# Float32 scores in pairs of heads from head 18 on, and another order of the opening phase

## The chip, the cores and the metric

The kernel runs on one core of one Trainium2 chip. The metric is the device time of one execution in microseconds (us), here the median of three runs. A profiled execution is a run of its own, and its time is given beside the median.

## What is computed

Three blocks follow one another: causal attention over blocks of 64 positions (8 batches, 8 heads, 576 positions, 64 features a head), a mixer block (a rank-32 mixing over positions, then a two-layer perceptron of width 2048 with a residual), and a gated output block.

```python
scores = scale * q @ k.T                      # per head, 576 x 576, blocks above the diagonal masked
attn = softmax(scores); x = attn @ v          # heads side by side: (8, 576, 512)
u = x + ((x.T @ U) @ V).T                     # mixing over positions
x = u + relu(u @ w_ch1) @ w_ch2               # 512 -> 2048 -> 512
gate = sigmoid(causal_conv5(x, conv_w))
out = (gate * (x @ w_val)) @ w_out
```

q, k, v are float32; the weights `w_ch1` and `w_ch2` come in 64 bits and are turned into pairs of float32 values in the kernel.

## The kernel before

**Stages.** The 64 heads (8 batches of 8) are numbered n. Phase 1 handles attention alone, for heads 0 to 10, and the mixing of batch 0. Then come nine groups of 512 tokens, each with 16 steps f of the perceptron: `emit_h1` (12 matmuls of 512 columns, lines 854 to 872) and `emit_o` (12 matmuls, lines 874 to 903). Each of them calls `gap()` twice, and `gap()` takes some steps of the attention stream for the heads of the next batch. The last stage is the gated output block (from 1329 us on).

**The attention stream.** `attention()` runs `tick(n)` for each head: four pieces of the scores (`emit_q_bank` for n under `NQ` = 18, `emit_s_piece` from 18 on), the maximum, then the product with v of head n-2 (`emit_pv`), the exponentials, and `emit_est` of head n-1. A pair of heads is normed in `emit_norm_a/b` and mixed by `mix_T`, `mix_G` and `mix_H` at fixed delays (`TPOS`, `GPOS`, `HPOS`; for batch 0 `T0`, `G0`, `H0`).

**Scores from head 18 on.** `prep_qk` (line 368) makes from the transposed tq and tk of a head three single-pass (float32r) operands: `ks` (the high part of k on both halves of the partitions), `kl` (its low part, the other half zero) and `qs` (high and low part of q). That is three ACT copies, one POOL memset and two POOL subtractions of 64x576 a head. `emit_s_piece` then does two float32r matmuls over all 128 rows for each part, into one PSUM bank, and one ACT copy (line 402) to SBUF. A float32 matmul, as in `emit_q_bank` (line 432) and for heads under 18 in `emit_pv` (line 612), appears in the trace as two MATMUL instructions.

**PSUM.** Four banks (`ps_p`) hold in turn everything but the four accumulators of `emit_o`: h1, the score pieces, the product with v, transposes and mixing. The order of TensorE's instructions is that of the program; the other engines' order is set at build time by priority, where an earlier line goes first and `tc.high_priority()` lifts what is inside.

**Weight blocks.** 32 calls of `split_w1` and `split_w2` (line 799 on) load 512 KB each, turn it to float32 on ACT, DVE (lines 124, 126, 127, 145: tile `wa`) and POOL, and for w2 store it again. Four of them (`PRE` = 2) are issued ahead of the first head, ten come in phase 1 at every 8th step of the stream, the other 18 in group 0, two a step f.

Of the kernel before, what the change touches and what calls it, by code (L numbers as in the profile page):

```python
# [8 lines left out]
F32 = mybir.dt.float32  # L9
F32R = mybir.dt.float32r  # L10
# [7 lines left out]
P = 128  # L18
# [4 lines left out]
def attn_moe_gate_kernel(ctx: ExitStack, tc: tile.TileContext, q, k, v, U, V, w1, w2, wval, convw, wout, out):  # L23
# [25 lines left out]
    LEAD = 2  # L49
    GATE = True  # L50
    GATE0 = False
    C0 = 6
    C1 = 8
    CMAX = 32
    LOWP = 0
    ABUF = 4
    RAWB = 2
    WAB = 2
    QV = 10
    KV = 0  # L60
    UVE = 0
    HPOS = 8
    GPOS = 6
    TPOS = 5
    PRE = 2
    CV0 = 1
    CV1 = 3
    MX0 = 0
    TP0 = 0
    NR0 = 0  # L70
    MM0 = 0
# [1 line left out]
    PR0 = 0  # L73
    CWAIT = 4
    NQ = FIRST_SPLIT
    MORE = 1
    T0 = 5
    G0 = 7
    H0 = 9
    NPART = 0  # L80
    PAT = (0,1)
    URG = True
# [4 lines left out]
    def f32(ap):  # L87
        return ap if ap.dtype == F32 else ap.bitcast(F32)
# [3 lines left out]
    def hi_act(o, i):  # L92
        act.copy(o, i)  # L93
# [4 lines left out]
    def lo(eng, o, i, h):  # L98
        eng.tensor_tensor(o, i, f32(h), op=ALU.subtract)  # L99
# [204 lines left out]
    def setup_att():  # L304
        for t in vstk:
            pool.memset(t[:, :, D:P], 1.0)
            pool.memset(t[0:D, NK - 1, :], 0.0)
        for a in range(2):
            for t in kz:
                pool.memset(t[a][own[1 - a]], 0.0)  # L310

    raw = {}

# [23 lines left out]
    stk = {}  # L337

    own = [slice(0, D), slice(D, P)]
    def pads(nm, dtype):  # L340
        return [st_p.tile([P, S], dtype, tag=f"{nm}{a}", name=f"{nm}{a}") for a in range(2)]

    kz = [pads(nm, F32) for nm in ("ks", "qs")]
    ks, qs = [], []
    kl = st_p.tile([P, S], F32R, name="kl")
    qkt = {}

    def prep_t(pn):
        if pn >= B * NP:
            return  # L350
        t = raw.pop(pn)
        if 2 * pn < NQ:
            tq = rot("tk" if pn % 2 else "tq", 1)
            z = kz[pn % 2]
            for rows in own if pn == 0 else (slice(0, P),):
                vec.transpose(tq[rows], t["q"][rows])
                for a in range(2):
                    if pn or rows == own[a]:
                        vec.transpose(z[a][own[a]], t["k"][own[a]])
            qkt[pn] = (tq, z)  # L360
        else:
            tq, tk = rot("tq", 1), rot("tk", 1)
            vec.transpose(tq, t["q"])
            vec.transpose(tk, t["k"])
            qkt[pn] = (tq, tk)
        load_qk(pn + 1)

    def prep_qk(n):
        if n >= B * H or n < NQ:
            return  # L370
        if not ks:
            ks.extend(pads("ks", F32R))
            qs.extend(pads("qs", F32R))
        tq, tk = qkt[n // 2]
        a = n % 2
        me, ot = own[a], own[1 - a]
        hi_act(qs[a][me], tq[me])
        hi_act(ks[a][me], tk[me])
        hi_act(ks[a][ot], tk[me])
        pool.memset(f32(kl[ot]), 0.0)  # L380
        lo(vec if n < KV else pool, kl[me], tk[me], ks[a][me])
        lo(vec if n < QV else pool, qs[a][ot], tq[me], qs[a][me])

    def kslice(j):
        return slice(q0[j], q0[j] + P) if q0[j] + P <= S else slice(S - P, S)

    stt = {}

    def emit_s_piece(n, i):
        pr, a = divmod(n, 2)  # L390
        if i == 0:
            stt[n] = [s_p.tile([P, w], F32, tag=f"s{h}", name=f"s{h}") for h, w in enumerate(sw)]
        ps = psum["a"].tile([P, 512], F32, tag="a", name="pS")
        o = 0
        for j, a0, a1 in pieces[i]:
            w = a1 - a0
            pe.matmul(ps[:, o:o + w], ks[a][:, kslice(j)], qs[a][:, a0:a1], start=True, stop=False)  # L397
            pe.matmul(ps[:, o:o + w], kl[:, kslice(j)], qs[a][:, a0:a1], start=False, stop=True)  # L398
            o += w
        j, a0, a1 = pieces[i][0]  # L400
        d = soff[j] + a0 - q0[j]
        act.copy(stt[n][half_of[j]][:, d:d + o], ps[:, 0:o])  # L402


    qbanks = [
# [14 lines left out]
    def emit_q_bank(n, i):  # L420

        a = n % 2
        tq, z = qkt[n // 2]
        if i == 0:
            s0, s1 = (s_p.tile([P, w], F32, tag=f"s{h}", name=f"s{h}") for h, w in enumerate(sw))
            eqs[n] = {3: s0[:, 0:4 * P], 1: s0[:, 4 * P:6 * P], 0: s1[:, 0:P], 2: s1[:, P:4 * P], 4: rot("m" if a else "mb", 1)}
            t = tiny_p.tile([P, 2 * NTT + 2], F32, tag="rq", name="rq")
            qmax[n] = (t[:, 0:NTT + 1], t[:, NTT + 1:], psum["a"].tile([P, 512], F32, tag="a", name="pS"))
        r, nm, _ = qmax[n]
        ps = psum["a"].tile([P, 512], F32, tag="a", name="pS") if i else _  # L430
        for t, k0, k1, o in qbanks[i]:
            pe.matmul(ps[:, o:o + k1 - k0], tq[:, kslice(t)], z[a][:, k0:k1], start=True, stop=True)
        if i == 0:
            vec.memset(ps[0:D, 4 * P - D:4 * P], MASKED)
        elif i == 2:
            vec.memset(ps[0:D, 3 * P - D:3 * P], MASKED)
        elif i == 3:
            vec.memset(ps.rearrange("p (c w) -> p c w", w=D)[0:D, 1:6:4, :], MASKED)
        for t, k0, k1, o in qbanks[i]:
            c = t + (k0 > 0)  # L440
            vec.reduce_max(r[:, c:c + 1], ps[:, o:o + k1 - k0], axis=AX.X)
        if i == 0:
            x = vec.tensor_scalar(nm[:, 3:4], r[:, 3:4], -scale, None, op0=ALU.mult)
        elif i == 2:
            vec.tensor_tensor(r[:, 4:5], r[:, 4:5], r[:, 5:6], op=ALU.max)
            x = vec.tensor_scalar(nm[:, 2:5:2], r[:, 2:5:2], -scale, None, op0=ALU.mult)
        elif i == 3:
            x = vec.tensor_scalar(nm[:, 0:2], r[:, 0:2], -scale, None, op0=ALU.mult)
        if i == 1:
            eqs[n]["wait"] = ps  # L450
            return
        noted(1, x)
        noted(3, x)
        for t, k0, k1, o in qbanks[i] + (qbanks[1] if i == 2 else []):
            src = eqs[n]["wait"] if i == 2 and t == NTT - 1 and k0 == 0 else ps
            act.activation(eqs[n][t][:, k0:k1], src[:, o:o + k1 - k0], AF.Exp, bias=nm[:, t:t + 1], scale=scale)
# [95 lines left out]
    def emit_est(n):  # L552

        if not 0 <= n < NH:
            return
        if n < NQ:
            emit_q_turn(n)
            return
        ss = stt.pop(n)
        for half, s in enumerate(ss):  # L560
            skip = 0 if half else WHOLE
            if half == 0:
                ef = late["e"].tile([P, WHOLE], F32, tag="ef", name="ef")
                act.activation(ef, s[:, 0:WHOLE], AF.Exp, scale=scale)
            eh = late["e"].tile([P, sw[half] - skip], F32R, tag=f"eh{half}", name="eh")
            hi_act(eh, s[:, skip:])
            el = e_p.tile([P, sw[half]], F32R, tag=f"e{half}", name="el")[:, skip:]
            lo(vec, el, s[:, skip:], eh)
            est[n, half] = (eh, el, ef, skip)
# [128 lines left out]
    def mix_H(pn, i):  # L698
        pcs = mix_pieces(pn // NP)
        if i >= len(pcs):  # L700
            return
        gi, a0, a1, off = pcs[i]
        if gi >= 2 and gi > y_done[0] + 2:
            later.append((pn, i))
            return
        xt = xts[pn]
        d = pn % NP
        uh, ul = u_tiles(gi)
        w = a1 - a0
        ps = ps_p.tile([P, 512], F32, tag="a", name="pH")  # L710
        pe.matmul(ps[:, 0:w], gst[pn], vst[:, a0:a1], start=True, stop=True)
        with behind(MX0 if pn < NP else 0):
            vec.tensor_tensor(xt[:, a0:a1], ps[:, 0:w], xt[:, a0:a1], op=ALU.add)
        hi_act(uh[:, d, off:off + w], xt[:, a0:a1])
        lo(pool, ul[:, d, off:off + w], xt[:, a0:a1], uh[:, d, off:off + w])
# [7 lines left out]
    def tick(n, mixed, last=B * NP):  # L723
# [5 lines left out]
        load_v(e + 1)  # L729
        for i in range(4):  # L730
            if n < NQ:
                emit_q_bank(n, i)
            elif new:
                emit_s_piece(n, i)
            if i == 3 and new and n >= NQ:
                emit_corners(n)
                emit_max_a(n)
            yield
        if new:
            if n >= NQ:  # L740
                emit_max_b(n)
            if n % 2 == 1:
                prep_t((n + 1) // 2)
            prep_qk(n + 1)
        yield from mixing(2 * e, mixed, last)
        if new and n >= NQ:
            for _ in emit_max_c(n):
# [261 lines left out]

    load_qk(0)  # L1010
    act.activation(cw[0:1, 0, 0:1], unit[0:1, 0:1], AF.Exp)
    for f in range(PRE):
        split_w1(f)
        split_w2(f)
    setup_att()
    prep_t(0)
    prep_qk(0)
    pb1 = ExitStack()
    pbp = {}

# [13 lines left out]
        pbp["ps"] = pb1.enter_context(tc.tile_pool(name="pbps", bufs=2, space=PSUM, side="right"))  # L1034

    stream = attention()
    convs = [(fn, f) for f in range(PRE, NF) for fn in (split_w1, split_w2)]

    def conv(n):
        where[0] = CV0 if gated_conv[0] else CV1  # L1040
# [131 lines left out]
```

## Time and profile before

| | us |
|---|---|
| median of 3 runs (1531.53 to 1535.98) | 1533.32 |
| the profiled execution | 1538.09 |
| its span, first to last instruction | 1536.3 |
| first perceptron matmul | 127.5 |
| start of group 1 | 314.9 |
| end of attention, about | 1154 |
| start of the gated output block | 1329 |

A row of the chain or the timeline gives start, duration, engine, line, operation, output<-inputs, shape and count; what stands in brackets is how long the engine sat idle before, and what ended that. In a row of stretches the stretch's length is followed by each engine's busy time, the granted TensorE clock (1.00 is 2.4 GHz, half of it 1.2 GHz) and the share of the DMA engines.

### The profile page before, as it was taken

Reading aid. Unit: us, or ns where it says so; the run is one execution under the profiler, and the core shown is the slowest. Engines: PE = TensorE matmul, PEld = TensorE weight load, DVE = VectorE, ACT = ScalarE, POOL = GpSimd, SP = SyncE. Lnnn points to the kernel's source line nnn. Section 1 sums busy time; section 2 is a strip of 40 time slices with the busy share of each in tenths; the row PEclk is TensorE's granted clock in tenths of the full one; section 3 lists DMA queues with packets and bytes.
Section 4 is the critical chain, followed back from the end, with each engine's and each line's share of the span. In section 5 each row is a group of like instructions: output and inputs, shape, how many; then the busy total and the mean of one; then the engine's idle time right before and its main releaser. Section 6 shows DMA issues by size and latency. Waiting matters only on the chain. (4 is left out here: it accounts for less than half of the span.)

```text
span 1536.3 us, 20391 instructions
## 1 busy us (share of the span) xinstructions
PE 1427.0 (93%) x6664; PEld 1151.1 (75%) x6664; DVE 1146.3 (75%) x2252; ACT 789.5 (51%) x1639; POOL 516.1 (34%) x587
## 2 busy tenths in 40 slices
PE   5897899979989998999899989989999999999999
PEld 2665677868767787777687778768888888778887
DVE  7887874659887888788888878887624427399991
ACT  4785565546565665666476556655512212243432
POOL 3133232333435333534443444335104210353410
PEclk8998999989999999999999999999999999999999
DMA  7555662224233333333323333232225543323221
GB/s 171 142 133 167 204 194 79 79 80 103 79 81 114 85 86 105 92 79 89 109 79 90 92 92 93 78 85 90 77 83 198 174 135 123 105 68 103 78 74 69
DMA packets 246291, 163.58 MB, mean 106 GB/s; under 512 B 197669, under 2 KB 212261, under 8 KB 246186
## 3 DMA queue, kind: packets, MB, share of 16 engines
q1 hardware_dynamic: 246186, 162.29, 36.6%
q8 instruction: 53, 0.87, 0.2%
q14 instruction: 52, 0.43, 0.1%
HBM read 134.98 MB, written 27.26 MB: 106 GB/s over the span
## 5 line engine op out<-in xcount | busy, mean ns | idle before, releaser
L887 PE MATMUL acc<-hh,w 128*128 128x512 f32 x1152 | 408.4, 405 | 10.2 <-ACT hh L869 10.2
L887 PEld LDWEIGHTS acc<-hh,w 128*128 128x128 f32 x1152 | 220.7, 192 | 57.7 <-ACT hh L869 12.8
L841 PE MATMUL h<-uh,w1hi 128*128 128x512 f32 x576 | 239.1, 415 | 9.9 <-DVE hl L870 6.3
L887 PE MATMUL acc<-hl,w 128*128 128x512 f32 x576 | 230.2, 400 | 5.9 <-DVE hl L870 5.9
L841 PE MATMUL h<-uh,w1lo 128*128 128x512 f32 x576 | 228.2, 396 | 0.0
L841 PE MATMUL h<-ul,w1hi 128*128 128x512 f32 x576 | 228.0, 396 | 0.0
L870 DVE SCALAR_TENSOR_TENSOR hl<-h,hh 128x512 fp32r<-128x512 f32 x144 | 98.2, 682 | 116.1 <-ACT hh L869 115.4
L869 ACT ACTIVATE hh<-h 128x512 fp32r<-128x512 f32 x144 | 85.8, 596 | 154.3 <-PE h L841 147.4
L550 ACT ACTIVATE s<-s 128x448 f32<-128x448 f32 x92 | 65.5, 712 | 150.0 <-DVE s L528 149.0
L841 PEld LDWEIGHTS h<-uh,w1hi 128*128 128x128 f32 x576 | 110.7, 192 | 35.8 <-DVE hl L870 8.2
L402 ACT COPY s<-pS 128x320 f32<-128x320 f32 (+2 forms) x184 | 89.8, 490 | 80.9 <-PE pS L398 77.2
L887 PEld LDWEIGHTS acc<-hl,w 128*128 128x128 f32 x576 | 110.5, 192 | 27.5 <-DVE hl L870 8.2
L841 PEld LDWEIGHTS h<-uh,w1lo 128*128 128x128 f32 x576 | 109.7, 190 | 24.8
L841 PEld LDWEIGHTS h<-ul,w1hi 128*128 128x128 f32 x576 | 110.7, 192 | 18.3 <-issue 1.4
L528 DVE TENSOR_TENSOR s<-s,mb 128x64 f32<-128x64 f32 (+4 forms) x230 | 123.0, 598 | 1.3
L962 DVE SCALAR_TENSOR_TENSOR gt<-yb,cw,gt 128x516 f32<-128x516 f32 (+1 forms) x144 | 116.5, 839 | 1.4
L99 POOL TENSOR_TENSOR vlo<-vstk,vhi 128x320 fp32r<-128x320 f32 x46 | 54.3, 1180 | 161.1 <-ACT vhi L93 148.1
L99 POOL TENSOR_TENSOR yl<-yb,yh 128x512 fp32r<-128x512 f32 (+7 forms) x64 | 67.7, 1091 | 96.9 <-ACT yh L93 96.8
L99 POOL TENSOR_TENSOR ul<-xt,uh 128x512 fp32r<-128x512 f32 (+7 forms) x64 | 53.2, 840 | 132.6 <-ACT uh L93 131.9
L397 PE MATMUL pS<-qs,ks 128*128 128x320 f32 (+4 forms) x276 | 80.4, 309 | 6.3 <-ACT lt L614 4.2
L398 PE MATMUL pS<-qs,kl 128*128 128x320 f32 (+4 forms) x276 | 82.4, 302 | 0.0
L99 DVE TENSOR_TENSOR el<-s,eh 128x448 fp32r<-128x448 f32 x92 | 76.7, 859 | 5.2 <-issue 4.6
(152 smaller groups left out, 3105.5 us busy)
## 6 DMA issues: line engine op xcount, KB each, us to landing
w<-w_s SPq DMA_DIRECT2D x144, 512.0 KB, 3.2
rawq<-in_q_dram SPq DMA_DIRECT2D x128, 72.0 KB, 2.4
rawk<-in_k_dram SPq DMA_DIRECT2D x128, 72.0 KB, 2.5
out_dram<-ot SPq DMA_DIRECT2D x35, 256.0 KB, 2.0
raw<-in_moe_w_ch_dram SPq DMA_DIRECT2D x64, 128.0 KB, 2.3
raw<-in_moe_w_ch_dram SPq DMA_DIRECT2D x16, 512.0 KB, 4.2
vstk<-in_v_dram SPq DMA_DIRECT2D x64, 128.0 KB, 2.6
w_s<-wo SPq DMA_DIRECT2D x16, 512.0 KB, 3.6
```

What stands on the lines that cost most here:

```text
L99: eng.tensor_tensor(o, i, f32(h), op=ALU.subtract)
L397: pe.matmul(ps[:, o:o + w], ks[a][:, kslice(j)], qs[a][:, a0:a1], start=True, stop=False)
L398: pe.matmul(ps[:, o:o + w], kl[:, kslice(j)], qs[a][:, a0:a1], start=False, stop=True)
L402: act.copy(stt[n][half_of[j]][:, d:d + o], ps[:, 0:o])
L528: noted(3, vec.tensor_tensor(sv(n, j), sv(n, j), mb[:, q0[j]:], op=ALU.subtract))
L550: act.activation(s, s, AF.Exp, scale=scale)
L841: pe.matmul(ps[:, 0:n], w[:, d, fs], x[:, d, 0:n], start=(d == 0 and i == 0), stop=(d == ND - 1 and i == 2))
L869: act.activation(hh[:, 0:n], ps[:, 0:n], AF.Relu)
L870: latest[0] = vec.scalar_tensor_tensor(hl[:, 0:n], ps[:, 0:n], 0.0, f32(hh[:, 0:n]), op0=ALU.max, op1=ALU.subtract)
L887: pe.matmul(acc[d][:, 0:n], w[:, wi, ds], x[:, 0:n], start=(f == 0 and i == 0), stop=(f == NF - 1 and i == 2))
L962: vec.scalar_tensor_tensor(gt[d][:, 0:gw], y[:, d, j:j + gw], cw[:, d, j:j + 1], gt[d][:, 0:gw], op0=ALU.mult, op1=ALU.add)
```

## The change

From head 18 on the scores are float32 matmuls over 64 rows: head 2p on partitions 0 to 63, head 2p+1 on 64 to 127, in turn for each part, each head into a bank of its own. All four pieces of both heads are issued in the tick of the even head; the odd head's tick has none, and starts its corners and maximum in its first step. `prep_qk` is gone. The score tiles of every third head lie in the buffers `za` and `zb`, which earlier hold the zero-padded k. The chain of `emit_q_bank` and `emit_q_turn` and the add in `mix_H` get high priority. No weight block is issued ahead of the first head; in phase 1 one comes at step 4 and then at every 12th step. Phase 1 has 12 heads (`MORE` = 2), and the mixing of batch 0 (`T0`, `G0`, `H0` = 4, 6, 7) lies wholly inside its ticks.

```diff
-    C0 = 6
-    C1 = 8
+    C0 = 4
+    C1 = 12
-    PRE = 2
-    MORE = 1
-    T0 = 5
-    G0 = 7
-    H0 = 9
+    MORE = 2
+    T0 = 4
+    G0 = 6
+    H0 = 7
...
-    def emit_s_piece(n, i):
-        pr, a = divmod(n, 2)
+    def emit_s_piece(pn, i):
+
+        heads = (2 * pn, 2 * pn + 1)
+        tq, tk = qkt[pn]
         if i == 0:
-            stt[n] = [s_p.tile([P, w], F32, tag=f"s{h}", name=f"s{h}") for h, w in enumerate(sw)]
-        ps = psum["a"].tile([P, 512], F32, tag="a", name="pS")
+            for n in heads:
+                stt[n] = [spare(("za", "zb")[h], w) if n % 3 == 1 else s_p.tile([P, w], F32, tag=f"s{h}", name=f"s{h}") for h, w in enumerate(sw)]
+        ps = [psum["a"].tile([P, 512], F32, tag="a", name="pS") for _ in own]
         o = 0
         for j, a0, a1 in pieces[i]:
             w = a1 - a0
-            pe.matmul(ps[:, o:o + w], ks[a][:, kslice(j)], qs[a][:, a0:a1], start=True, stop=False)
-            pe.matmul(ps[:, o:o + w], kl[:, kslice(j)], qs[a][:, a0:a1], start=False, stop=True)
+            for t, me in zip(ps, own):
+                pe.matmul(t[:, o:o + w], tk[me, kslice(j)], tq[me, a0:a1], start=True, stop=True)
             o += w
         j, a0, a1 = pieces[i][0]
         d = soff[j] + a0 - q0[j]
-        act.copy(stt[n][half_of[j]][:, d:d + o], ps[:, 0:o])
+        for n, t in zip(heads, ps):
+            act.copy(stt[n][half_of[j]][:, d:d + o], t[:, 0:o])
...
         if n < NQ:
-            emit_q_turn(n)
+            with tc.high_priority():
+                emit_q_turn(n)
...
-        with behind(MX0 if pn < NP else 0):
+        with tc.high_priority():
             vec.tensor_tensor(xt[:, a0:a1], ps[:, 0:w], xt[:, a0:a1], op=ALU.add)
...
             if n < NQ:
-                emit_q_bank(n, i)
-            elif new:
-                emit_s_piece(n, i)
-            if i == 3 and new and n >= NQ:
+                with tc.high_priority():
+                    emit_q_bank(n, i)
+            elif new and n % 2 == 0:
+                emit_s_piece(n // 2, i)
+            if i == (0 if n % 2 else 3) and new and n >= NQ:
                 emit_corners(n)
                 emit_max_a(n)
...
-            prep_qk(n + 1)
...
-    for f in range(PRE):
-        split_w1(f)
-        split_w2(f)
-    prep_qk(0)
-    convs = [(fn, f) for f in range(PRE, NF) for fn in (split_w1, split_w2)]
+    convs = [(fn, f) for f in range(NF) for fn in (split_w1, split_w2)]
```

## Rows read from the trace of the kernel before

**Rows 1.** The page: busy time of TensorE, and its busy tenths in 40 slices.

```profile
PE 1427.0 (93%) x6664; PEld 1151.1 (75%) x6664; DVE 1146.3 (75%) x2252; ACT 789.5 (51%) x1639; POOL 516.1 (34%) x587
PE   5897899979989998999899989989999999999999
```

**Rows 2.** Stretches: length; busy PE, PEld, DVE, ACT, POOL; clock, DMA share, GB/s.

```profile
0.00:36.50 36.50, 17.57 (x52) 9.91 (x53) 28.14 (x63) 15.32 (x30) 10.77 (x22) 0.86 0.75 173
36.50:118.50 82.00, 75.52 (x380) 51.53 (x379) 71.58 (x218) 63.13 (x155) 21.24 (x19) 1.00 0.56 141
...
127.50:190.00 62.50, 52.11 (x210) 38.68 (x209) 51.13 (x105) 34.02 (x70) 19.30 (x15) 0.89 0.67 200
...
314.90:1154.00 839.10, 783.37 (x3801) 649.73 (x3800) 673.71 (x1316) 482.12 (x987) 323.00 (x395) 0.98 0.32 89
```

**Rows 3.** Timeline of TensorE from 20 to 41 us.

```profile
21.76 4.41 PE L432 MATMUL pS<-ks,tq 128*128 128x512 f32 x10 [8.04 <-DVE ks L359]
...
32.45 4.19 PE L432 MATMUL pS<-qs,tk 128*128 128x512 f32 x10 [3.79 <-ACT m L456]
36.48 2.98 PE L612 MATMUL pPV<-e,vstk 128*128 128x128 f32 x12
39.29 0.38 PE L472 MATMUL pE<-ident,m 128*128 128x128 f32 x2
```

**Rows 4.** DVE's work on the weight blocks (tile wa) in three stretches: length, busy time.

```profile
0.00:36.50 36.50, 13.61 (x21) 0.86 0.75 173
36.50:118.50 82.00, 23.26 (x47) 1.00 0.56 141
127.50:220.00 92.50, 42.04 (x66) 0.92 0.68 203
```

**Rows 5.** Timeline of TensorE from 118 to 128 us, the end of phase 1.

```profile
122.04 1.44 PE L688 MATMUL pG<-x,ust 128*128 128x256 f32 x5 [3.25 <-DVE x L99]
126.90 0.82 PE L711 MATMUL pH<-vst,g 128*128 128x512 f32 x2 [3.42 <-DVE g L99]
```

**Rows 6.** Timeline of TensorE from 520 to 528 us: score pieces between perceptron matmuls.

```profile
521.13 0.19 PE L397 MATMUL pS<-qs,ks 128*128 128x64 f32 x1
...
521.81 0.39 PE L887 MATMUL acc<-hh,w 128*128 128x512 f32 x1
522.04 0.40 PE L887 MATMUL acc<-hl,w 128*128 128x512 f32 x1
...
524.88 0.37 PE L397 MATMUL pS<-qs,ks 128*128 128x448 f32 x1
...
525.29 0.40 PE L841 MATMUL h<-uh,w1hi 128*128 128x512 f32 x1
```

**Rows 7.** Timeline of TensorE around the only matmuls over few rows (5 rows).

```profile
1179.23 0.39 PE L887 MATMUL acc<-hh,w 128*128 128x512 f32 x1
1179.55 0.41 PE L277 MATMUL pC<-unit,wa 5*128 5x5 f32 x4
1179.89 0.50 PE L841 MATMUL h<-uh,w1hi 128*128 128x512 f32 x1
1180.23 0.40 PE L841 MATMUL h<-ul,w1hi 128*128 128x512 f32 x1
```

**Rows 8.** Groups of instructions by form: work of `prep_qk` (busy us, mean ns).

```profile
L99 POOL TENSOR_TENSOR qs<-tq,qs 64x576 fp32r<-64x576 f32 x46 | 70.4, 1531 | 27.1 <-PE pPV L612 18.9 <-ACT qs L93 5.7
L99 POOL TENSOR_TENSOR kl<-tk,ks 64x576 fp32r<-64x576 f32 x46 | 65.8, 1431 | 9.3 <-ACT ks L93 6.2
L93 ACT CAST ks<-tk 64x576 fp32r<-64x576 f32 x92 | 61.7, 671 | 8.5 <-PE pS L397 6.0 <-DVE tk L364 1.4
```

**Rows 9.** Line 516, a DVE copy of 32x18: least, median and greatest ns.

```profile
L516 DVE COPY r<-r x46: 166/168/1904, 285.3 to 1093.6; 32x18 f32<-32x18 f32 x46
```

**Rows 10.** Waits of TensorE, 314.9 to 1154 us: the longest in total, times, longest.

```profile
PE pPV L612 <- DVE hl L870: 11.5, 5, 2.3
PE pT L680 <- DVE xt L713: 8.4, 5, 3.1
```

More of the change, by code (lines that the diff above doesn't have):

```diff
@@ L58, in attn_moe_gate_kernel @@
     WAB = 2
-    QV = 10
-    KV = 0
     UVE = 0
@@ L64, in attn_moe_gate_kernel @@
     TPOS = 5
-    PRE = 2
     CV0 = 1
     CV1 = 3
-    MX0 = 0
     TP0 = 0
@@ L309, in setup_att @@
             for t in kz:
-                pool.memset(t[a][own[1 - a]], 0.0)
+                pool.memset(t[own[1 - a], a, :], 0.0)
     raw = {}
@@ L339, in attn_moe_gate_kernel, with spare @@
     own = [slice(0, D), slice(D, P)]
[L340 to L345, printed above, removed]
+    def spare(nm, n):
+        return st_p.tile([P, n], F32, tag=nm, name=nm)
+    kz = [spare(nm, 2 * S).rearrange("p (a s) -> p a s", s=S) for nm in ("za", "zb")]
     qkt = {}
@@ L358, in prep_t @@
                     if pn or rows == own[a]:
-                        vec.transpose(z[a][own[a]], t["k"][own[a]])
+                        vec.transpose(z[own[a], a, :], t["k"][own[a]])
             qkt[pn] = (tq, z)
@@ L366, in prep_t @@
         load_qk(pn + 1)
[L368 to L382, printed above, removed]
     def kslice(j):
@@ L431, in emit_q_bank @@
         for t, k0, k1, o in qbanks[i]:
-            pe.matmul(ps[:, o:o + k1 - k0], tq[:, kslice(t)], z[a][:, k0:k1], start=True, stop=True)
+            pe.matmul(ps[:, o:o + k1 - k0], tq[:, kslice(t)], z[:, a, k0:k1], start=True, stop=True)
         if i == 0:
```

## The prediction, made before the changed kernel ran

> **What bounds the kernel now.** I read the page's first two parts, then stretches, then the timeline where the stretches show a loss. TensorE is busy 93% of the span, and its row of tenths is at 9 almost everywhere but in the first five slices [rows 1]. So a microsecond more on TensorE costs about one after 127 us, and there is something to gain for nothing only at the front and in TensorE's waits. The stretches say how much [rows 2]. In the first 36.5 us TensorE works 17.6 while DVE works 28.1: the softmax chain on DVE sets the pace. From 36.5 to 118.5 TensorE has 75.5 of 82 us and DVE 71.6: about equal. In the stage with split heads (314.9 to 1154 us) TensorE has 783.4 of 839.1 us, so 55.7 idle, and a mean clock of 0.98, so some 17 us more lost at half clock: 73 us of slack, while DVE is busy 80%. The last stage and the groups without attention are not touched.
>
> **The sum** is made against the profiled execution, 1538.09 us (span 1536.3), which is 4.77 over the median of 1533.32. I carry the difference over to the median.
>
> **1. The opening, no blocks ahead of the first head.** The first product with v starts at 36.48 us, after waits of 8.04 and 3.79 us on TensorE [rows 3]. Of DVE's 28.1 busy us there, 13.6 are weight blocks [rows 4, 2], and they sit between the maxima on which the exponentials, and with them the PSUM banks for the next scores, wait. One block (about 2.3 us, from 23.26 us for ten [rows 4]) is left, at step 4, and it now stands behind the chain. SP loses the loads of four blocks ahead of the second pair's q and k, which also lands those earlier. I take -10 us; bounds 0 (the chain waits on loads instead) and -14.
>
> **2. Phase 1 at a lower rate of blocks, chain in front.** Ten blocks cost DVE 23.3 of its 71.6 us [rows 4, 2]; at every 12th step it is two thirds. TensorE is idle 6.5 of the 82 us, the ceiling. I take -4, bounds 0 and -6.5.
>
> **3. The end of phase 1.** The mixing of the last pair runs bare: G waits 3.25 us and H 3.42 [rows 5]. Now the fourth pair's T, G and H stand in ticks with other matmuls between them. I take -7 (6.7, and a little clock), bounds -3 and -8: the wait of the first h1 on the last u tile stays.
>
> **4. Head 11 moves** from group 0 into phase 1. Its TensorE work is the same in both places: 0, bounds -1 and +1.
>
> **5. Group 0.** From 127.5 to 190 us TensorE is idle 10.4 us and its clock is 0.89 [rows 2], where 18 blocks stand in DVE's order with the chain (42 us [rows 4]). Now 25 blocks come here, still two a step, so the density is the same but lasts to step 11 instead of 7, and the chain passes them. The blocks are five steps ahead of the h1 that needs them, which hides them. If that cover went, late blocks would stop TensorE at each step, and the tiles of heads 18 on, which take over the blocks' buffers after the last one, would come late. I take -5, bounds -12 and +8.
>
> The front: -10 - 4 - 7 - 5 = **-26 us**, bounds -41 and +6.
>
> **6. TensorE's time for the scores, heads 18 to 63, 23 pairs.** Before, slots from one score piece to the next matmul: 0.68 us (three parts, 512 columns) and 0.41 (448), so 0.29 by width for each piece of 320 [rows 6]; 1.67 a head, 3.34 a pair. Float32 over the full array: the product with v has the same 1600 columns in 12 instructions, and from its start to the next group 2.81 us pass [rows 3], 0.88 ns a column for each of the two instructions of a float32 matmul. If the heads' matmuls run one after another a pair costs 5.62 us; wholly side by side, 2.81. No row shows two matmuls at once, so both ends stand. I take the overlap that program order leaves: in the rows of TensorE matmuls start in order, and a matmul's second instruction must follow its first on the same rows. So A, A', B, B' take three slots where four would stand, A' beside B. The one-part pieces of 320, 448 and 320 columns cost 3 x 0.88 ns x 1088 = 2.87 us, and in the three-part piece B' also runs beside the next A, so 0.06 + 0.06 + 0.17 + 0.17 + 3 x 0.225 = 1.13: 4.0 us a pair.
>
> Going from 128 rows to few and back shows once: a matmul at 1179.23 should be followed 0.23 us later as in [rows 6], and the 5-row one starts after 0.32; coming back, the second wide one starts 0.34 after the first [rows 7]. That is 0.09 + 0.11 = 0.20 us for in and out, four times a pair: 0.8, bounds 0 and 0.8.
> The Trainium skill, "TensorEngine Tiling (Array Packing)", section Key Properties, speaks against this change here: "Changing tiling mode (not just tile) drains the TensorE". Of it [rows 7] give one instance, with 5 rows and not 64; by the rule the 0.8 stands, and without it the sum below would be 18 us lower. The same list says that different tiles can load weights and multiply in parallel, which no run here shows.
>
> So 4.8 for 3.34: +1.46 x 23 = **+34 us**; bounds (2.81 - 3.34) x 23 = -12 and (6.42 - 3.34) x 23 = +71.
>
> **7. What `prep_qk` frees.** POOL loses two subtractions of 1.43 to 1.53 us a head, ACT three copies of 0.67 [rows 8]. Both are off the path. But DVE's small copy in line 516 takes 166 ns at least and 1904 at most [rows 9], and since nothing in DVE's own order stands inside one instruction, I put the long ones down to POOL's work beside it. So DVE would get time back within the chain, and the add of `mix_H` no longer stands behind the five subtractions of the softmax. TensorE's longest waits in this stage are on just these DVE results (hl, xt) [rows 10]. Of the 73 us of slack I take half, **-37**; bounds 0 and -60.
>
> **8. Two banks at once.** Each of 92 steps now takes two of the four banks, and they are freed by two ACT copies in a row, while h1 holds a third. The next step, half an h1 (six slots of 0.23 us [rows 6]) later, needs two again. Queued behind those copies on ACT is the relu on which the next `emit_o` waits. In odd ticks there is nothing. I take 0.1 us a step, **+10**; bounds 0 and +30.
>
> Sum: -26 + 34 - 37 + 10 = **-19 us**, so 1519 for the profiled execution and **1514** for the median.
>
> **Rivals.**
> *No overlap:* the two row halves run one after another. A pair costs 5.62 + 0.8 and step 6 is +71: -26 + 71 - 37 + 10 = +18, **1551**, slower. It decides from 3.34 + (26 + 37 - 10) / 23 = 5.64 us a pair on. For it: nothing in the trace runs two matmuls at once. Against: the two share no rows and no bank, and no semaphore stands between them.
> *Full overlap,* 2.81 + 0.8 a pair: step 6 is +6, so -47, **1486**. For it: weight loads run beside matmuls throughout (75% beside 93% [rows 1]), so the order of issue may be no bound. Against: the second instruction on the same rows.
> *The banks eat the relief:* step 7 gives 0 and step 8 costs 30: -26 + 34 + 30 = +38, **1571**. For it: the longest waits today, of the product with v and of pT, stand where a new bank is begun [rows 10]. Against: ACT has 92 us less to do in copies of this kind and the odd tick to catch up.
> *The change doesn't do what it says at the front:* the first heads wait for q and k, or the chain, though in front, for POOL. Steps 1 to 5 give 0: **1540**. Against: DVE is the busiest engine there, half of it with blocks.
>
> **How the numbers follow.** Forecast 0.41, full overlap 0.25, no overlap 0.20, banks 0.08, front 0.06. The forecast's own range is 1497 to 1532. What a measurement can tell from no change is 0.3%, 4.6 us, so 1528.7 to 1537.9. Faster: 0.25 + 0.37 of the forecast and 0.01 of the front case = 0.63. Same: 0.03 + 0.02 + 0.02 of no overlap = 0.07. Slower: 0.18 + 0.08 + 0.03 + 0.01 = 0.30. The range goes from 1480 to 1555: it leaves out a third of full overlap (relief near its bound) and, above, the banks' case and the end of no overlap.
>
> **What would show it.** Step 1: the first line-612 matmul at about 26 us in place of 36.5. Step 3: no wait of 3 us before G and H. Step 6: from the first score matmul of a 448-column piece to the next perceptron matmul: 1.2 us and a little if half overlapped, 0.8 if wholly, 1.6 if not at all. The rows of line 472, or a wide matmul behind a score piece, show whether coming back costs 0.1. Step 7: line 516's greatest time falls, and the groups 1 to 5 shrink or not. Step 8: waits of score matmuls or h1 on ACT's line 402 copy. The prediction is wrong if the piece's time falls at the other end, or if the waits on hl and xt stay as they are.

## The result, and the profile after

The changed kernel takes **1516.82 us** in the median of four runs (1514.38 to 1518.09) where the kernel before takes 1532.98 beside it: a ratio of **0.989**, 95% interval 0.9871 to 0.991. That is faster, and 3 us from the 1514 forecast. But of the sum only the total holds: the front was to give 26 us and gave 5 at most, and the paired scores with all that follows from them were to cost 7 and gave 14 to 17.

The profiled execution took 1518.09 us (span 1516.3). The page, busy times and the rows of tenths for TensorE and its clock:

```profile
PE 1430.9 (94%) x6664; PEld 1106.4 (73%) x6664; DVE 1088.6 (72%) x2249; ACT 703.7 (46%) x1501; POOL 349.0 (23%) x449
PE   5889899979998998999899989999999999999999
PEclk9999899989999999999999999999999999999999
```

GpSimd falls most, and TensorE's row still has dents to the end of the attention: we come to them. Now the stretches, as in [rows 2]. First two of the kernel before that were not shown, phase 1 to its end and group 0; then after, cut at the first product with v, the first perceptron matmul, and the starts of group 1 and of group 7:

```profile
36.50:127.50 91.00, 77.85 (x388) 53.22 (x387) 76.87 (x230) 68.42 (x167) 23.50 (x22) 0.96 0.53 136
127.50:314.90 187.40, 171.77 (x780) 130.97 (x778) 130.59 (x280) 105.58 (x221) 59.51 (x55) 0.96 0.50 144
```

```profile
0.00:28.70 28.70, 15.74 (x51) 9.40 (x52) 19.34 (x52) 10.71 (x23) 6.44 (x19) 0.94 0.62 118
28.70:130.30 101.60, 87.85 (x427) 59.24 (x425) 77.50 (x230) 70.18 (x171) 18.89 (x18) 0.97 0.46 112
130.30:313.20 182.90, 166.85 (x751) 123.30 (x751) 138.65 (x294) 99.32 (x213) 52.50 (x51) 0.96 0.58 170
313.20:1134.10 820.90, 783.88 (x3788) 607.14 (x3787) 615.89 (x1312) 405.43 (x860) 171.70 (x268) 0.97 0.34 91
```

Read length minus TensorE's busy time. The opening is idle 13.0 us instead of 18.9, and shorter by 7.8. Phase 1 is idle 13.75 instead of 13.15, with one head more in it (10.0 us of TensorE's time). Group 0 is idle 16.05 instead of 15.6. So only the opening gained. At group 1 the kernel is 1.7 us ahead (313.2 for 314.9), and 3.8 of the scores' higher price already lies before that point: two pairs at 4.42 us are done there, where it was three heads at 1.67. In these two profiles the front itself thus gave 5.5 us; experiment 4 shows that one profile can be off by as much. The split-head stage went from 839.0 to 820.9 us: idle 37.0 us for 55.7, VectorE 616 us busy for 674, GpSimd 172 for 323. The rest of the program is unchanged.

The scores, timeline of TensorE where [rows 6] stood:

```profile
517.07 0.39 PE L870 MATMUL acc<-hh,w 128*128 128x512 f32 x1
517.39 0.81 PE L379 MATMUL pS<-tq,tk 64*128 64x320 f32 x4
518.13 0.50 PE L824 MATMUL h<-uh,w1hi 128*128 128x512 f32 x1
518.46 0.39 PE L824 MATMUL h<-ul,w1hi 128*128 128x512 f32 x1
...
519.72 1.02 PE L379 MATMUL pS<-tq,tk 64*128 64x448 f32 x4
520.67 0.50 PE L824 MATMUL h<-uh,w1hi 128*128 128x512 f32 x1
```

One row "x4" is a whole piece: two heads, two instructions each. The records inside the first start at 517.389, 517.396, 517.762 and 517.769: the two heads run side by side, in both passes. From the 448-column piece to the next perceptron matmul 0.95 us pass, close to the 0.8 of whole overlap and far from 1.2 or 1.6. But going in and out is dear: the piece starts 0.32 after the wide matmul in place of 0.23, takes 0.74 where two passes of 320 columns at 0.88 ns are 0.56, and the second wide matmul behind it comes 0.33 after the first in place of 0.23. Together 0.37, as much for the piece of 448 columns, and 0.48 for the one of three parts. The change of rows makes most of it, not float32: in group 0 of the kernel before, a float32 piece of 448 columns on the full array (line 432) between the same wide matmuls has 0.23, 0.78 and 0.32 us for these three times, and by the same sum only 0.09 too much. Over all pieces of the stage the added time is 0.93, 1.15, 0.93 and 1.38 us, **4.4 a pair** for 3.34.

The small copy of [rows 9], in the stage (first the kernel before, then after; busy, mean ns), and the waits of TensorE there, as in [rows 10]:

```profile
L516 DVE COPY r<-r 32x18 f32<-32x18 f32 x44 | 39.2, 891 | 1.4
```

```profile
L494 DVE COPY r<-r 32x18 f32<-32x18 f32 x44 | 17.9, 408 | 1.4
```

```profile
PE pT L663 <- DVE xt L696: 29.1, 5, 6.1
PE pT L655 <- DVE xt L696: 7.9, 1, 7.9
```

The waits on hl are gone, and the many short ones on xt too; one stop in each group, of 6 to 8 us, holds all that is left, 37.0 us on xt where [rows 10] and one of 6.4 us made 14.8. TensorE runs some 7 us or more at half clock behind each.

### The profile page after: what moved, and what is told of

It is laid out like the page before. It is cut to its first block, busy times and chain, and to the rows that moved or that the text cites. A ratio compares the mean times of both kernels' runs of the same rounds, so it can differ in the third digit from the quotient of the medians.

```text
span 1516.3 us, 20089 instructions
## 1 busy us (share of the span) xinstructions
PE 1430.9 (94%) x6664; PEld 1106.4 (73%) x6664; DVE 1088.6 (72%) x2249; ACT 703.7 (46%) x1501; POOL 349.0 (23%) x449
## 4 chain that ended last, share of the span: by engine, by line
PE 76%; DVE 15%; ACT 3%; DMA 2%; issue 2%; SPq 1%; POOL 1%; DVEq 0%; ACTq 0%; POOLq 0%
PE h L824 23%; PE acc L870 23%; PE pPV L595 8%; PE o L987 7%; PE pS L379 6%; PE val L963 5%; DVE rq L423 1%; DMA raw<-in_moe_w_ch_dram 1%; PE pG L671 1%; DVE s L510 1%; DVE y L882 1%; DVE wa L123 1%; DVE m L474 1%; PE pS L414 1%; DVE r L484 1%
## 5 line engine op out<-in xcount | busy, mean ns | idle before, releaser
L824 PE MATMUL h<-uh,w1hi 128*128 128x512 f32 x576 | 242.6, 421 | 2.6 <-ACT s L438 1.7
L95 POOL TENSOR_TENSOR vlo<-vstk,vhi 128x320 fp32r<-128x320 f32 x46 | 43.1, 936 | 372.2 <-ACT vhi L89 353.4
L379 PE MATMUL pS<-tq,tk 64*128 64x320 f32 (+4 forms) x552 | 92.4, 429 | 1.7 <-ACT s L384 1.7
L384 ACT COPY s<-pS 128x512 f32<-128x512 f32 (+2 forms) x124 | 58.2, 496 | 48.5 <-PE pS L379 47.2
L596 ACT COPY xt<-pPV 64x128 f32<-64x128 f32 (+1 forms) x128 | 50.1, 392 | 65.6 <-PE pPV L595 63.8
L532 ACT ACTIVATE s<-s 128x448 f32<-128x448 f32 (+1 forms) x62 | 44.1, 711 | 73.6 <-DVE s L510 73.5
L510 DVE TENSOR_TENSOR s<-s,mb 128x64 f32<-128x64 f32 (+4 forms) x155 | 71.4, 524 | 0.3
L379 PEld LDWEIGHTS pS<-tq,tk 64*128 64x128 f32 x552 | 42.1, 185 | 35.8 <-issue 21.9
```

The costliest lines, as they stand in the source:

```text
L379: pe.matmul(t[:, o:o + w], tk[me, kslice(j)], tq[me, a0:a1], start=True, stop=True)
L384: act.copy(stt[n][half_of[j]][:, d:d + o], t[:, 0:o])
L510: noted(3, vec.tensor_tensor(sv(n, j), sv(n, j), mb[:, q0[j]:], op=ALU.subtract))
L824: pe.matmul(ps[:, 0:n], w[:, d, fs], x[:, d, 0:n], start=(d == 0 and i == 0), stop=(d == ND - 1 and i == 2))
```

## The experiments

**1. Each half of the change alone.** The paired scores in the old front, with `C0`, `C1`, `MORE`, `PRE`, `T0`, `G0` and `H0` as before and without the three priorities, of which one stands here:

```diff
-                with tc.high_priority():
-                    emit_q_bank(n, i)
+                emit_q_bank(n, i)
```

> The kernel before with the paired scores alone (and with them the end of prep_qk); the blocks, the ticks of the mixing, and every priority stay as before. Theory from the two traces: the split-head stage shrinks from 839 to about 821 us, because the relief is larger than the dearer scores, and the front stays as it was: 18 us less, ratio 0.988. The rival is the sum as it was predicted (the gain lies in the front, scores and relief together cost 7 us): ratio 1.005. A third case, that the relief needs the high priority of the add in mix_H as well, lies between: 5 to 10 us less, 0.994 to 0.997.

Measured: 1518.7 beside 1535.3, **0.9891** (0.9878 to 0.9903). The stage takes 819.9 us. All of the change's gain is in the scores, and the high priority of the add in `mix_H` has no part in it.

The new front with the old scores (the reverse edit, on the kernel before):

> The kernel before with the front alone: no blocks ahead, one at each 12th step from step 4, the softmax chain of heads 0 to 17 at high priority, twelve heads in phase 1 and the earlier ticks of the last pair's mixing. The scores of heads 18 on and prep_qk as before. Theory from the two traces: the first product with v comes 8 us earlier, the first perceptron matmul about 3 us later with one head more behind it, and group 0 gives that back: 0 to 4 us less in all, ratio 0.997 to 1.000. The rival is the sum as predicted: 26 us less, ratio 0.983.

Measured: 1529.81, **0.9965** (0.9951 to 0.9979): 5.4 us less, a fifth of what was predicted and a little more than I expected from the two traces. That it is near the 5.5 of the stretches is chance: in this run's own profile group 1 starts at 319.1 us, later than before (314.9), and the gain lies in the split-head stage, 831.3 us with the same old scores for 839.0. And the two halves don't add: 0.9891 and 0.9965 would make 0.9856, and the whole change has 0.989 (0.9871 to 0.991). Beside the new scores no gain of the front is seen.

**2. Is it the overlap?** Both heads on the same 64 rows:

```diff
-            for t, me in zip(ps, own):
+            for t, me in zip(ps, (own[0], own[0])):
```

> The changed kernel, with one word altered: the second head's score matmuls read rows 0 to 63, as the first head's do, so that no two of them can run beside one another. Each second head gets the scores of the first, so the output is not the reference's; the count, the shapes and the banks are as in the changed kernel. Theory (the two heads overlap wholly, a pair costs 4.42 us): a pair loses one whole half, 2.8 us, so 23 pairs cost 65 us more than the changed kernel, about 1582, ratio 1.032. If the half overlap of the prediction were right, 23 x 1.6 = 37 us more, 1554, ratio 1.013. If there were no overlap, nothing changes: 1517, ratio 0.989. From the first score matmul of a 448-column piece to the next perceptron matmul: 1.9 to 2.0 us in place of 1.16.

Measured: 1578.36, **1.0273** (1.0252 to 1.0294), so 59 us above the changed kernel, 2.6 a pair. Its timeline of TensorE:

```profile
535.69 1.34 PE L379 MATMUL pS<-tq,tk 64*128 64x320 f32 x4
536.96 0.50 PE L824 MATMUL h<-uh,w1hi 128*128 128x512 f32 x1
...
538.55 1.77 PE L379 MATMUL pS<-tq,tk 64*128 64x448 f32 x4
540.25 0.50 PE L824 MATMUL h<-uh,w1hi 128*128 128x512 f32 x1
```

The piece of 320 columns takes 1.27 for 0.74 us, that of 448 takes 1.70 for 0.95. The heads overlap wholly; half an overlap would have given 37 us by the sum above, and the measured 59 are near the 65 of the whole. Without it the change would have been slower than the kernel before.

**3. Where does the relief come from?** GpSimd's part of `prep_qk` put back as dead work:

```diff
+    dum = spare("zc", S)
+        pool.memset(dum[ot], 0.0)
+        pool.tensor_tensor(dum[me], tk[me], tq[me], op=ALU.subtract)
+        pool.tensor_tensor(dum[ot], tq[me], tk[me], op=ALU.subtract)
...
+            pool_work(n + 1)
         yield from mixing(2 * e, mixed, last)
```

> The changed kernel with prep_qk's work on GpSimd put back as dead work: for each head from 18 on one memset and two subtractions of 64 x 576 into a spare tile that nobody reads. Theory (the relief is VectorE's, which no longer runs beside GpSimd's subtractions): VectorE's time above its own 10th percentile in this stage goes from 50 back towards 100 us, the longest small copies from under 0.5 back to over 1 us, and the time grows by 10 to 30 us: 1527 to 1547, ratio 0.996 to 1.009. Rival (the relief is that of ScalarE's three copies a head, or of the shorter chain from the score to its use): VectorE's short instructions grow, but the time stays within 4 us of 1517, ratio 0.987 to 0.991.

Measured: 1581.3, **1.0297** (1.028 to 1.0315): 63 us, twice what the theory allowed. Its direction holds and its size doesn't. Then the same queue without the long reads:

```diff
-        pool.tensor_tensor(dum[me], tk[me], tq[me], op=ALU.subtract)
-        pool.tensor_tensor(dum[ot], tq[me], tk[me], op=ALU.subtract)
+        pool.tensor_tensor(dum[me][:, 0:1], tk[me][:, 0:1], tq[me][:, 0:1], op=ALU.subtract)
+        for _ in range(6):
+            pool.memset(dum[ot], 0.0)
```

> As the run with GpSimd's dead work, but with the two subtractions of 64 x 576 (1.58 and 1.64 us) replaced by six memsets of 64 x 576 (0.57 us each, so 3.4 us for 3.2) and one subtraction of 64 x 1, which keeps the reads of the new q and k. GpSimd's queue is as long as there, but none of the long instructions reads two inputs. Theory (what costs is VectorE running beside GpSimd's subtractions): the time falls from 1581 back to within 8 us of the changed kernel, 1517 to 1525, ratio 0.989 to 0.994. Rival (what costs is GpSimd's queue, where the corners of the next head stand behind the dead work): it stays near 1575 to 1585, ratio 1.026 to 1.032.

Measured: 1527.07, **0.9976** (0.9956 to 0.9996), 13 us above the changed kernel beside the same runs (0.989 of 1531.19 is 1514) and, by the ratio, 5 above the theory's range. In the profile 6 us lie ahead of group 1, where dead work has hardly begun; its start varies as much between profiles. The stage of each kernel, the subtractions first, then the memsets:

```profile
318.90:1198.00 879.10, 811.71 (x3788) 612.71 (x3787) 676.95 (x1315) 401.91 (x860) 333.07 (x388) 0.96 0.33 85
```

```profile
319.10:1145.90 826.80, 782.71 (x3789) 605.67 (x3788) 626.27 (x1311) 404.82 (x860) 342.95 (x587) 0.97 0.34 91
```

GpSimd is as busy in one as in the other (333 and 343 us), but only the subtractions stretch the stage (879 us; the changed kernel 821, the memsets 827) and VectorE's busy time (677; 616; 626). So it is VectorE beside GpSimd's reads, and not GpSimd's queue. A memset is shorter than a subtraction (0.58 us for 1.6), so the length of one GpSimd instruction could be the cause as well; the traces speak against it for VectorE's instructions with two inputs. The maximum over 192 columns (lines 485 and 484) takes 0.36 us in the median, and never more, in the 33 cases beside memsets alone, and 1.46 in the 28 beside subtractions alone; over 320 columns it is 0.49 (31 cases) and 1.26 (26).

For each form of VectorE's instructions I summed the time above the 10th percentile of its duration, 327 to 1030 us: 122 us before, 52 after, 99 with the subtractions, 59 with the memsets. Sorted by the GpSimd instruction that overlaps most, 49 of the 122 stand beside `prep_qk`'s own instructions and 31 beside another, the add into xt in line 632. That add still runs in the changed kernel, but no VectorE instruction is held up beside it any more. So part of the relief came from where the rest of GpSimd's work happens to fall. What ScalarE's three copies have in it was not run. The dead work costs more than `prep_qk` did (39 us, below) for the same 3 us a head; 44 of the 99 are in the three maxima of line 484, beside which it happens to fall. Why that place costs so much more was not tried.

**4. The front, undone part by part** (each against the changed kernel's 0.989). One profile can't tell a few us here: in five kernels with the same front, group 1 starts between 313.2 and 319.1 us. So the medians count, and a difference of two of them is good to 4 or 5 us. In what follows the waits on lt are TensorE's transposes waiting for ScalarE's copies of the product with v, over the whole of phase 1: 8.9 us in the changed kernel. The chain of heads 0 to 17 without high priority:

> The changed kernel without the high priority of the softmax chain of heads 0 to 17 (scores, maxima, exponentials and turns in program order); blocks, ticks, paired scores and the add of mix_H as in the changed kernel. Theory from the trace of the changed kernel: in phase 1 the exponentials, put in front, wait on ScalarE for VectorE's factors and hold up the copies of the product with v behind them, on which TensorE's transposes wait (8.8 us in 28.7 to 119 us, where before there were 3.9 in 82); in turn, those waits fall to about 4 us, and the time is 0 to 5 us less than the changed kernel: 1512 to 1517, ratio 0.986 to 0.989. Rival (the priority does what it was costed for): phase 1 and group 0 grow, 3 to 10 us more, ratio 0.991 to 0.996.

Measured: 1514.56, **0.9894** (0.9874 to 0.9915). No difference that can be told, and the waits on lt stayed (9.6 us): the theory that the priority makes them falls. The old rate of blocks (`C0 = 6`, `C1 = 8`):

> The changed kernel with the old rate of blocks after the opening (the first at step 6, then one at each 8th step), so that about 10 in place of 7 are done in phase 1 and about 22 in place of 25 in group 0. Theory (the work of the blocks is on VectorE's path wherever it stands; group 0 gave back what the front gained): phase 1 grows by 3 to 5 us and group 0 shrinks by as much: within 3 us of the changed kernel, 1514 to 1520, ratio 0.987 to 0.991. Rival (the later blocks are what holds group 0 at 183 us): group 0 shrinks by 8 or more and phase 1 does not grow: 1509 or less, ratio 0.984 or less.

Measured: 1515.92, **0.9897** (0.9876 to 0.9919). No difference here either; the waits on lt are 10.2 us. The old ticks (`T0, G0, H0 = 5, 7, 9`):

> The changed kernel with the ticks of the mixing in phase 1 as before (T, G and H of a pair at 5, 7 and 9 half steps in place of 4, 6 and 7); still twelve heads, blocks and priorities as changed. In the changed kernel T and G stand ahead of the products with v of their tick: TensorE waits 2.4 us for GpSimd's xt, ScalarE waits up to 2.25 us for VectorE's sum of G with the copies of the product with v queued behind it, and the transposes wait 8.9 us on those copies. Theory (the new ticks pay for the covered end of phase 1 with waits inside it): the waits on lt fall to 4 to 5 us and those on xt go, while the bare G and H come back with 3 us each in 119 to 135 us: the sum stays, within 3 us of the changed kernel, ratio 0.987 to 0.991. Rival (the waits come from the head start alone and the ticks are a pure gain): 4 to 8 us slower than the changed kernel, ratio 0.992 to 0.995.

Measured: 1522.03, **0.9923** (0.9902 to 0.9943), some 5 us slower. The waits on lt stayed here too (10.3 us), so the ticks don't make them either, and H stands bare again, for longer than in [rows 5]:

```profile
138.44 0.82 PE L694 MATMUL pH<-vst,g 128*128 128x512 f32 x2 [6.68 <-DVE g L95]
```

Four blocks ahead of the first head again (`PRE = 2`, all else as changed):

> The changed kernel with four weight blocks ahead of the first head again, as before; all else as changed, so group 0 has 21 blocks in place of 25. Undone alone so far: the rate of the blocks (1516) and the priority of the chain (1515) cost nothing, the old ticks some 5 us. Theory (the opening's gain is given back in group 0, where the four blocks now come): the first product with v moves from 28.7 back to about 36 us, the first perceptron matmul is 5 to 8 us later, group 0 shrinks by as much, and the whole stays within 3 us of the changed kernel, ratio 0.987 to 0.991. Rival (the opening's gain lasts to the end, as step 1 of the prediction had it): 6 to 10 us slower than the changed kernel, ratio 0.993 to 0.996.

Measured: 1522.33, **0.993** (0.9905 to 0.9954), some 6 us slower: in this kernel the opening's gain lasts. The intervals of these last two overlap that of the changed kernel a little, so 5 and 6 us are only just clear of nothing. And the first run of experiment 1 undoes these parts all together, and the priority of the add, at no cost (0.9891). So a part undone alone tells what it is worth beside the others, not what it gives by itself.

**5. The stop at the end of each group.** What VectorE does while TensorE stands, timeline of the changed kernel (rows of other work and of VectorE's small instructions left out):

```profile
460.69 0.25 PE L694 MATMUL pH<-vst,g 128*128 128x192 f32 x1
461.48 0.60 ACT L852 ACTIVATE hh<-h 128x512 fp32r<-128x512 f32 x1
461.79 0.68 DVE L882 TENSOR_TENSOR y<-acc,uh 128x512 f32<-128x512 f32 x1
462.39 2.08 DVE L510 TENSOR_TENSOR za<-za,mb 128x192 f32<-128x192 f32 x2
462.56 1.31 POOL L883 TENSOR_TENSOR y<-y,ul 128x512 f32<-128x512 f32 x1 [4.36 <-DVE y L882]
463.83 1.37 POOL L95 TENSOR_TENSOR vlo<-vstk,vhi 128x320 fp32r<-128x320 f32 x1
464.40 1.68 DVE L510 TENSOR_TENSOR zb<-zb,mb 128x448 f32<-128x448 f32 x2
466.31 1.49 DVE L95 TENSOR_TENSOR el<-s,eh 128x448 fp32r<-128x448 f32 x2
467.72 0.68 DVE L882 TENSOR_TENSOR y<-acc,uh 128x512 f32<-128x512 f32 x1
468.32 0.34 DVE L696 TENSOR_TENSOR xt<-pH,xt 128x192 f32<-128x192 f32 x1
468.72 0.42 PE L663 MATMUL pT<-ident,xt 128*64 128x128 f32 x1 [5.93 <-DVE xt L696]
```

The product pH is there at about 461; the add that empties its bank comes after eleven other instructions in VectorE's order and ends at 468.7. Two of the subtractions are long: the one over 576 columns takes 1.82 us and the one over 448 takes 1.28, where alone they take 0.75 and 0.62 (medians); GpSimd's two instructions stand beside them. My first thought was the buffer of y, the tile of a group's result:

```diff
-        late["y"] = lpool("yp", 2)
+        late["y"] = lpool("yp", 3)
```

> The changed kernel with three buffers in place of two for the y tiles at the end of a group. In the changed kernel TensorE stops once in each group for 6 us (37 us in six stops), on the add of mix_H, which stands on VectorE behind an add into a y tile whose buffer is still being sent out, and each stop is followed by some 6.8 us at half clock. Theory: with a third buffer the stop shortens from 6 to 2 to 3 us, and the half clock behind it shrinks: 3 to 5 us a group, 15 to 30 us in all, 1487 to 1502, ratio 0.970 to 0.980. Rival (the stop is GpSimd's add into y or the end of the acc matmuls, not the buffer): 0 to 3 us less, ratio 0.987 to 0.989.

Measured: 1521.61, **0.9938** (0.9914 to 0.9962): slower, against both theories. The stops grew, to 7.5 us. In its trace two adds into y now run back to back ahead of the maxima, and the chain behind them is later. VectorE has no idle time in the rows above, so the buffer held up nobody there, and what is left is VectorE's backlog. GpSimd's second add into y, moved to VectorE in groups 0 to 5:

```diff
-                pool.tensor_tensor(y[:, 0:n], y[:, 0:n], f32(ul[:, d, 0:n]), op=ALU.add)
+                (vec if g < 6 else pool).tensor_tensor(y[:, 0:n], y[:, 0:n], f32(ul[:, d, 0:n]), op=ALU.add)
```

> The changed kernel with one word altered: in groups 0 to 5 the second add into y (y + ul) runs on VectorE in place of GpSimd. The buffer of y was shown not to be what holds VectorE up at the end of a group. Theory: it is VectorE's backlog, and 17.9 us of it in 327 to 1030 us are instructions that run beside GpSimd's add into y (five groups, 3.6 us each); four adds of some 0.6 us more on VectorE cost 2.4 us a group. So VectorE gains about 1 us a group, and with it the stop of 6 us shortens by 0 to 2 us: 0 to 12 us less than the changed kernel, 1505 to 1517, ratio 0.981 to 0.989. Rival (VectorE's own work is what counts, beside GpSimd or not): the stop grows by 2 us a group, 8 to 14 us slower, ratio 0.994 to 0.998.

Measured: 1500.12, **0.9786** (0.9761 to 0.981), better than expected: VectorE got *more* work and the kernel takes 16 us less. In the split-head stage VectorE's busy time fell from 616 to 608 us, with 23 instructions more. And both adds on TensorE, with the copy on ScalarE:

```diff
+            if f == NF - 1 and g < 6:
+                for x in ut[g]:
+                    pe.matmul(acc[d][:, 0:n], identr, x[:, d, 0:n], start=False, stop=False)
...
-                vec.tensor_tensor(y[:, 0:n], acc[d][:, 0:n], f32(uh[:, d, 0:n]), op=ALU.add)
-                pool.tensor_tensor(y[:, 0:n], y[:, 0:n], f32(ul[:, d, 0:n]), op=ALU.add)
+                    act.copy(y[:, 0:n], acc[d][:, 0:n])
```

> The changed kernel in which, for groups 0 to 5, uh and ul are added to acc on TensorE (two matmuls with an identity for each of four banks, 8 x 0.23 = 1.84 us a group) and ScalarE copies acc into y: both adds into y are gone from VectorE (4 x 0.68 us a group) and GpSimd (4 x 1.50). Theory (VectorE's backlog at the end of a group makes the stop of 6 us and the half clock behind it): VectorE has 2.7 us and the 3.6 us beside GpSimd's adds less to do, so the stop goes almost wholly, some 5 us and 2 to 3 us of clock a group, less the 1.84: 3 to 6 us a group, 18 to 36 in all, 1481 to 1499, ratio 0.966 to 0.978. Rival (the order of VectorE's instructions, not the backlog, keeps the add of mix_H behind the five subtractions): the stop stays near 5 us and the kernel is 2 to 11 us slower for the matmuls, ratio 0.990 to 0.996.

Measured: **1492.91**, **0.9727** (0.9705 to 0.975), as the theory had it, and the fastest version here: about 25 us below the changed kernel, 42 below the kernel before. Its stage, and the waits of TensorE in it:

```profile
311.60:1106.80 795.20, 782.86 (x3829) 605.70 (x3828) 577.77 (x1281) 414.60 (x882) 137.69 (x244) 1.00 0.36 94
```

```profile
PE h L827 <- ACT lt L600: 6.2, 6, 2.2
PE pT L666 <- DVE xt L699: 6.1, 5, 1.4
```

Idle 12.3 us for 37.0, a clock of 1.00 for 0.97, and as much busy time although it has 48 matmuls more in all.

## Why the number came out right, step by step

By the sign that the prediction set itself it is wrong: the time of a score piece, 0.95 us where 1.2 was forecast, stands for whole overlap. Only its total came out.

**Step 1 (opening, -10).** The mechanism holds at the front: the first product with v moved by 7.8 us. Undoing it alone costs some 6 at the end, undoing it with the rest of the front nothing.

**Step 2 (phase 1, -4).** Wrong. Of 82 us TensorE was idle 6.5 [rows 2]; of the 90.3 between 28.7 and 119 us it is now idle 12.5. The waits after, TensorE, 28.7 to 119 us:

```profile
PE pE L454 <- ACT lt L597: 8.8, 6, 2.3
PE pT L655 <- POOL xt L615: 2.4, 3, 0.9
PE pH L694 <- DVE xt L696: 1.4, 1, 1.4
```

I had costed VectorE's queue and not ScalarE's. One instance, timeline of VectorE, ScalarE and TensorE:

```profile
73.26 0.87 DVE L95 TENSOR_TENSOR x<-pT,x 128x512 fp32r<-128x512 f32 x2
74.06 0.15 DVE L428 TENSOR_SCALAR rq<-rq 128x2 f32<-128x2 f32 x1
74.24 0.58 ACT L438 ACTIVATE s<-pS,rq 128x384 f32<-128x384 f32 x1 [1.78 <-DVE rq L428]
...
77.17 0.53 ACT L597 COPY lt<-pPV 64x448 f32<-64x448 f32 x1
77.75 0.33 PE L454 MATMUL pE<-ident,m 128*128 128x128 f32 x1 [2.29 <-ACT lt L597]
```

An exponential waits for VectorE's factor, the copies that free the bank of the product with v are queued behind it on ScalarE, and the transposes wait. Neither the priority, nor the rate of the blocks, nor the ticks is the cause by itself: undone, each left these waits at 9 to 10 us over phase 1, and four blocks ahead left 7.4. What raised them from the 3.9 us of the kernel before stays open; the twelfth head was not undone alone.

**Step 3 (end of phase 1, -7).** Right in mechanism: the waits of [rows 5] are gone (1.2 us idle in the last 11), and undoing the ticks costs some 5 us.

**Step 4 (head 11, 0) and step 5 (group 0, -5).** TensorE's idle time in group 0 is as before, so -5 is wrong; it is about +1.7 (166.85 us busy, where 171.77 less 10.0 for the head and plus 3.8 for the scores gives 165.6, and 0.45 more idle). The parts don't add: undone alone in the changed kernel they cost 6, 5, 0 and 0 us, and together nothing; beside the old scores they bring 5.4. The old ticks under twelve heads leave H barer than before, so part of the ticks' 5 us is only what the moved head needs. The head alone was not run.

**Step 6 (scores, +34; measured +25).** Two errors that offset. The step that failed is "in the rows of TensorE matmuls start in order, and a matmul's second instruction must follow its first": the second passes pair up as the first do, so 4.0 us a pair were 2.8. And the switch, 0.20 by the one instance of [rows 7], is 0.40 with 64 rows, so 0.8 a pair were 1.6. The full-overlap rival had the mechanism and, with 0.8, the wrong size; its 1486 was off by this and by the front. The Trainium skill, "TensorEngine Tiling (Array Packing)", Key Properties, has both: tiles that run in parallel, and the drain at a change of mode. The trace agrees with both (starts 7 ns apart, and 0.37 to 0.48 us for each change in and back); the price is this case's.

**Step 7 (relief, -37).** Right in size, and in part by luck. In the stage 21 pairs cost 92.8 us for 71.8 of 43 heads, 21.0 more, and the stage is 18.1 shorter: a relief of **39**. Idle time fell by 18.7 of them; the other 20 are within TensorE's busy time, which stayed at 783 us with dearer scores. The starts of successive matmuls place them. A wide matmul's record lasts 0.39 us and the next one starts after 0.23, so a wait under 0.16 us leaves no idle time. Summed over the stage, and outside the scores, starts came later than at their usual distance by 10.4 us at full clock before and 1.8 after, and at half clock by 18.6 and 14.4; and the old score pieces took 78.4 us in all where 43 heads at 1.67 give 71.8. That is 19 of the 20: short waits and half clock. GpSimd was rightly named (experiment 3), but the sign that it was read from was not `prep_qk`'s: all 20 copies of line 516 that took over 1.3 us in the stage overlap the add into xt of line 632, which the change didn't touch. Of the waits named, those on hl went, and those on xt grew to one long stop a group. The add of `mix_H` still stands behind the five subtractions of the softmax, against step 7, and its priority had no part.

**Step 8 (two banks, +10).** Too much: in the stage TensorE's waits are on the add in `mix_H` alone, none on line 384's copies; in group 0 there is one, of 1.7 us.

So the total came out because the front's missing 20 us were made up by 9 in step 6, 8 to 10 in step 8 and 2 in step 7. That is luck. And this account is that of two profiles, 20.0 us apart; the medians are 16.2 apart, the profile before being one of the slowest of its kernel (its stage of 839.0 us was 831.3 in the other profile with the old scores). By the medians the scores alone gave 16.6 us, and the front beside them nothing that can be told.

## What to carry over

Two float32 matmuls on 64 rows each, next to one another in program order, run wholly side by side, but each change from the full array to such a pair and back costs 0.4 us here: count the changes, not only the columns. When TensorE waits for VectorE, look first at what GpSimd does beside it: here VectorE became faster when it took over GpSimd's work. And undo a change's parts together as well as one by one: here two parts were worth 5 and 6 us alone, and all of them together nothing.

## What the runs showed of the hardware

- The small VectorE copy (32x18) takes 164 ns alone and up to 1150 beside GpSimd's add of two tensors. GpSimd's memsets of the same total length cost the stage 6 us where subtractions cost 58. The Trainium skill, "SBUF — State Buffer", "SBUF: two separate sides", says that VectorE and GpSimd share a port pair that one of them holds for a whole instruction, and that a VectorE instruction with two inputs in SBUF contends only with a GpSimd instruction that reads SBUF. The memsets agree with the second half: beside them alone, maxima with two inputs took their usual time (0.36 us over 192 columns), and beside subtractions four times as long. Copies with one input suffer beside memsets as well: the 32x18 copy took up to 0.54 us beside memsets of 0.58.
- A float32 matmul's two instructions on 64 rows interleave with those of the other rows: 7 ns between the starts, 0.37 us to the second pass of 320 columns.
- A stop of 6 us on TensorE was followed by some 7 us at half clock (0.63 us a matmul where 0.39 is usual); in the last version, with waits of 2.2 us at most, the stage's clock was 1.00.
